# A gated GLU with a state-space branch on one core: first weight pair on two other rings, four pairs held back, and a start of single token tiles

## The chip, the cores and the metric

The kernel runs on one core of a Trainium2 chip. Times are device microseconds (us) of one execution. "Profiled span" is the time from the first to the last instruction in the one execution that was traced; the timed value is 1.7 to 2.1 us longer. TensorE's granted clock is recorded with each run (1.000 is full speed).

## The reference, cut to what matters

```python
xn = layernorm(x)                       # x: [2048 tokens, 576], bfloat16
glu = (sigmoid(xn @ w_gate) * (xn @ w_up)) @ w_down      # inner width 4608
# ... ssm: a diagonal complex state-space scan over the 2048 tokens
return x + ssm(xn) + glu
```

The gate, up and down products are most of the work, and all of it is TensorE's.

## The kernel before

Tokens come in blocks of 512 (four tiles of 128). The inner width comes in "groups" of 128 columns, and weights are loaded as pairs of groups: 288 KB of gate weights into the upper 64 partitions, 288 KB of up weights into the lower 64. 576 features are nine pieces of 64, so a group on one block is 18 matmuls of 64 rows, a gate and an up one side by side in the two halves of the array (in the trace of before 2628 of them fill 283.7 us, 108 ns each; the last warm-ups of 512 columns, over the whole array, come 216 ns apart).

The loads at the beginning. Two input tiles go on each of the SP and ACT rings (a ring is the queue on which one engine starts its DMA transfers); all weights, and block 1's input, go through GpSimd:

```python
for tt in range(TT_B):                                   # TT_B = 4: block 0
    load_x(tt, nc.sync if tt % 2 == 0 else nc.scalar)
for pr in range(2):
    load_wgu((0, pr), nc.gpsimd, nc.gpsimd)              # pairs 0 and 1
for tt in range(TT_B, 2 * TT_B):
    load_x(tt, nc.gpsimd, "hst")                         # block 1
dskip_rows = consts.tile([P, D], BF16, name="dskip_rows")
nc.gpsimd.dma_start(dskip_rows[:], A_Dskip.partition_broadcast(P))
for pr in range(2, 4):
    load_wgu((0, pr), nc.gpsimd, nc.gpsimd)              # pairs 2 and 3
```

The start, on block 0. Tiles are normalised, transposed on TensorE and copied to `xT` two at a time, and the first two groups are multiplied in 256-column halves:

```python
for tt in range(2):
    ln_stats(tt)
    ln_std(0, tt, tt + 1)
for tt in range(2):
    ln_recip(0, tt, tt + 1)
    ln_norm(tt, twice=False)
    start_transpose(tt)
busy(20, P)                                   # 20 warm-up matmuls on zeros
start_copy(0, slice(0, NH), nc.scalar.copy)
# ... cut: statistics of tiles 2 and 3, the copies of tile 1
start_groups[0].mms(slice(0, 2 * P))
start_transpose(2)
start_transpose(3)
start_groups[1].mms(slice(0, 2 * P))
# ... cut: the copies of tiles 2 and 3
for g in start_groups:
    g.mms(slice(2 * P, TB))
```

The order of the groups afterwards (`f` is the group, the second number the block), then the down-projection of both blocks, which reads `hT`, the product of a group's gate and up halves that VectorE writes. Block 1's input is normalised behind this and transposed by DMA:

```python
order = [(f, 0) for f in range(2, 8)] + [(f, 1) for f in range(0, 8)]
order += [(f, nb) for nb in range(2) for f in range(8, 12)]
```

## Time and profile before

| | before |
|---|---|
| time, median (range) of the runs that stand against the changed kernel | 509.75 us (508.93 to 509.82) |
| profiled span | 508.4 us |
| TensorE busy | 500.6 us |
| first gate/up matmul, first one of 512 columns | 8.63, 13.90 us |
| first down-projection matmul, end of the last matmul | 58.71, 504.46 us |

The page and the table of stretches are read in the prediction below. Two lines of the page that it did not show matter later: TensorE's granted clock in 40 slices of the span, in tenths, and the DMA queue that the page calls "instruction" (packets, MB, share of the 16 DMA engines).

```profile
PEclk9999999999999999999999999999999999999999
...
q8 instruction: 35, 0.57, 0.5%
```

The clock is whole wherever it is recorded, from 4.3 us on. (The page prints 9 before that too, but the first warm-up matmuls, of 512 columns, are 0.43 us apart, twice the later 0.216.) The second line looks like nothing: half a per cent of the DMA time.

### The profile page before, as it was taken

Reading aid. Unit: us, or ns where it says so; the run is one execution under the profiler, and the core shown is the slowest. Engines: PE = TensorE matmul, PEld = TensorE weight load, DVE = VectorE, ACT = ScalarE, POOL = GpSimd, SP = SyncE. Lnnn points to the kernel's source line nnn. Section 1 sums busy time; section 2 is a strip of 40 time slices with the busy share of each in tenths; the row PEclk is TensorE's granted clock in tenths of the full one; section 3 lists DMA queues with packets and bytes.
Section 4 is the critical chain, followed back from the end, with each engine's and each line's share of the span. In section 5 each row is a group of like instructions: output and inputs, shape, how many; then the busy total and the mean of one; then the engine's idle time right before and its main releaser. Section 6 shows DMA issues by size and latency. Waiting matters only on the chain.

```text
span 508.4 us, 10667 instructions
## 1 busy us (share of the span) xinstructions
PE 500.6 (98%) x4536; PEld 292.6 (58%) x4536; DVE 323.5 (64%) x703; ACT 204.6 (40%) x368; POOL 96.6 (19%) x143
## 2 busy tenths in 40 slices
PE   8989999999999999999999999999999999999996
PEld 5445676444477444467764444774444774446775
DVE  6964999977888587868688667786675222221111
ACT  4757642556500756530016655005655005553000
POOL 6147430133110043110001231100431001300000
PEclk9999999999999999999999999999999999999999
DMA  8997997075220098342340662200753201600001
GB/s 208 172 170 143 235 194 125 2 164 122 57 57 25 1 170 153 76 107 69 73 104 3 163 141 48 46 24 1 150 122 81 48 25 38 172 1 4 33 25 36
DMA packets 42960, 45.60 MB, mean 90 GB/s; under 512 B 30496, under 2 KB 34336, under 8 KB 42912
## 3 DMA queue, kind: packets, MB, share of 16 engines
q0 software_dynamic: 12672, 34.23, 31.7%
q1 hardware_dynamic: 29808, 10.33, 10.2%
q8 instruction: 35, 0.57, 0.5%
q10 hardware_dynamic: 432, 0.37, 0.2%
q14 instruction: 13, 0.11, 0.1%
HBM read 34.36 MB, written 2.36 MB: 72 GB/s over the span
## 4 chain that ended last, share of the span: by engine, by line
PE 94%; DVE 3%; DMA 1%; ACT 1%; issue 0%
PE pgu L488 52%; PE pd L562 35%; PE pbu L517 7%; DVE bnst L220 1%; DMA xT<-xn 1%; DVE xn L240 1%; DMA xt<-in_A_x_dram 1%; ACT xT L737 0%; DVE acc L263 0%; PE ptr L734 0%; DVE mv L221 0%; DVE tmpxd L260 0%; DVE hT L497 0%; DVE ob L571 0%; DVE xn L245 0%
## 5 line engine op out<-in xcount | busy, mean ns | idle before, releaser
L488 PE MATMUL pgu<-xT,wgu 64*128 64x512 bf16 (+1 forms) x2628 | 283.7, 373 | 1.8 <-DMA xT<-xn 1.8
L488 PEld LDWEIGHTS <-wgu 64*128 64x128 bf16 x2628 | 130.0, 94 | 150.7 <-issue 2.5
L562 PE MATMUL pd<-wd,hT 128*128 128x288 bf16 x1152 | 144.6, 286 | 0.0
L494 ACT ACTIVATE sT<-pgu 128x512 bf16<-128x512 f32 x144 | 86.5, 600 | 119.4 <-PE pgu L488 109.7
L562 PEld LDWEIGHTS <-hT 128*128 128x128 bf16 x1152 | 112.2, 98 | 30.7 <-issue 0.8
L497 DVE TENSOR_TENSOR hT<-sT,uT 128x512 bf16<-128x512 bf16 x144 | 60.5, 421 | 100.0 <-ACT uT L495 99.8
L495 ACT CAST uT<-pgu 128x512 bf16<-128x512 f32 x144 | 84.1, 584 | 0.0
L151 POOL DMA_DIRECT2D wgu<-in_B_w_gate_dram x36 | 27.7, 769 | 227.7 <-PE pgu L488 207.7
L523 ACT COPY bure<-pbu 128x512 f32<-128x512 f32 x16 | 9.4, 585 | 104.3 <-PE pbu L517 88.5
L157 POOL DMA_DIRECT2D wd<-in_B_w_down_dram x36 | 26.4, 735 | 100.6 <-PE pd L562 99.5
L582 DVE TENSOR_TENSOR acc<-acc,pd 128x576 f32<-128x576 f32 x32 | 23.9, 750 | 24.1 <-PE pd L562 24.1
L579 DVE TENSOR_TENSOR ob<-acc,pd 128x576 bf16<-128x576 f32 x15 | 11.3, 754 | 40.9 <-PE pd L562 40.9
L517 PE MATMUL pbu<-xT,bt 64*128 64x512 bf16 x288 | 33.7, 376 | 0.0
L562 PEld LDWEIGHTS <-hst 128*128 128x128 bf16 x288 | 28.2, 98 | 7.1
L151 POOL DMA_DIRECT2D wgu<-in_B_w_up_dram x36 | 26.7, 742 | 1.5 <-issue 0.8
L562 PE MATMUL pd<-ctre,hst 128*128 128x288 bf16 x128 | 26.6, 286 | 0.0
L562 PE MATMUL pd<-ctim,hst 128*128 128x288 bf16 x128 | 26.6, 286 | 0.0
L432 DVE TENSOR_TENSOR_SCAN gre<-r,g0re,wrim 128x512 bf16<-128x512 f32 x20 | 25.5, 1277 | 0.1
L517 PEld LDWEIGHTS <-bt 64*128 64x128 bf16 x288 | 13.7, 94 | 17.1 <-issue 0.9
L439 DVE TENSOR_TENSOR_SCAN gim<-r,g0im,wrim 128x512 bf16<-128x512 f32 x16 | 20.4, 1276 | 0.0
L220 DVE BATCH_NORM_STATS2 bnst<-xt 128x6 f32<-128x288 bf16 x32 | 12.5, 433 | 2.4 <-DMA xt<-in_A_x_dram 2.4
L419 DVE TENSOR_TENSOR tq<-T,buim 128x512 bf16<-128x512 bf16 x20 | 13.7, 684 | 0.0
(113 smaller groups left out, 273.9 us busy)
## 6 DMA issues: line engine op xcount, KB each, us to landing
wgu<-in_B_w_gate_dram POOLq DMA_DIRECT2D x36, 288.0 KB, 4.4
wgu<-in_B_w_up_dram POOLq DMA_DIRECT2D x36, 288.0 KB, 5.1
wd<-in_B_w_down_dram POOLq DMA_DIRECT2D x36, 288.0 KB, 6.2
out_dram<-ob SPq DMA_DIRECT2D x15, 144.0 KB, 1.8
xt<-in_A_x_dram SPq DMA_DIRECT2D x10, 144.0 KB, 2.6
xt<-in_A_x_dram POOLq DMA_DIRECT2D x4, 144.0 KB, 7.2
bt<-ctre POOLq DMA_DIRECT2D x2, 288.0 KB, 6.9
bt<-ctim POOLq DMA_DIRECT2D x2, 288.0 KB, 7.8
```

The source lines that it names most:

```text
L151: eng.dma_start(w[rows, :, :], src[:, fs].rearrange("(c p) f -> p c f", p=H))
L157: nc.gpsimd.dma_start(wd[:], B_w_down[f0:f0 + FP * P, :].rearrange("(n p) d -> p n d", p=P))
L220: nc.vector.bn_stats(st[:, gi, :], xt[:, gi * DH:(gi + 1) * DH])
L432: nc.vector.tensor_tensor_scan(gre[:], r_bc, w[:, 0, :], g0re[:, col], ALU.mult, ALU.add)
L439: nc.vector.tensor_tensor_scan(gim[:], r_bc, w[:, 1, :], g0im[:, col], ALU.mult, ALU.add)
L488: nc.tensor.matmul(self.ps[:, gi, cols], w[rows, c, fs], xT[self.nb][rows, c, cols], start=c == 0, stop=c == NH - 1)
L494: nc.scalar.activation(sT[:], self.ps[:, 0, :], ACT.Sigmoid)
L495: nc.scalar.copy(uT[:], self.ps[:, 1, :])
L497: nc.vector.tensor_mul(h[:], sT[:], uT[:])
L517: nc.tensor.matmul(out, w, xT[self.nb][rows, c, ts_], start=c == 0, stop=c == NH - 1)
L562: nc.tensor.matmul(out, lhsT, rhs[:, a * DH:(a + 1) * DH], start=i == 0, stop=i == n - 1)
L582: nc.vector.tensor_add(halves(acc[:]), halves(acc[:]), pd[:, :, 0:DH])
```

## The change

Its intent: the first useful matmul should come earlier, and the hole before block 1 should go. The first pair goes on the SP and ACT rings, behind block 0's input tiles. The next four pairs are held until tile 0's statistics are done, by a small write that VectorE makes into pair 1's buffer and that the load has to wait for. Tiles go through the start one at a time. Eight groups on block 0, not six, stand between the start and block 1. The fifth pair borrows the place of a table that is not needed yet.

```diff
+        if key == (0, 4):
+            w = consts.tile([P, NH, FP * P], BF16, name="wgu4", tag="T1")
+        # ... cut
+        if held:
+            nc.vector.memset(w[:, 0, 0:2], 0.0)
 ...
-    for pr in range(2):
-        load_wgu((0, pr), nc.gpsimd, nc.gpsimd)
+    load_wgu((0, 0), nc.sync, nc.scalar)
     for tt in range(TT_B, 2 * TT_B):
-        load_x(tt, nc.gpsimd, "hst")
+        load_x(tt, nc.sync, "hst")
 ...
+    def load_behind():
+        for pr in range(1, 5):
+            load_wgu((0, pr), nc.gpsimd, nc.gpsimd, held=pr == 1)
+        nc.gpsimd.dma_start(dskip_rows[:], A_Dskip.partition_broadcast(P))
 ...
+    ln_stats(0)
+    load_behind()
+    ln_std(0, 0, 1)
+    ln_stats(1, (0,))
+    start_norm(0)
+    start_transpose(0)
+    busy(14, P)
+    start_copy(0, CA, nc.scalar.copy)
+    # ... cut: the same for tiles 1 to 3, each tile's 128-column matmuls
+    #     on both groups between the transposes of the next tiles
 ...
-                order = [(f, 0) for f in range(2, 8)] + [(f, 1) for f in range(0, 8)]
-                order += [(f, nb) for nb in range(2) for f in range(8, 12)]
+                order = [(f, 0) for f in range(2, 10)] + [(f, 1) for f in range(0, 10)]
+                order += [(f, nb) for nb in range(2) for f in range(10, 12)]
# cut: prefetch counts for five pairs, side loads one step earlier in their round,
#      the state inputs asked for through the background list
```

More of the change, by code (lines that the diff above doesn't have):

```diff
@@ L144, with load_wgu @@
     wd_t = {}
-    def load_wgu(key, eng_g, eng_u):
+    def load_wgu(key, eng_g, eng_u, held=False):
         f0 = (key[0] % NC * (FC // FP) + key[1]) * FP * P
-        w = wpool.tile([P, NH, FP * P], BF16, name="wgu", bufs=4)
+        if key == (0, 4):
+            w = consts.tile([P, NH, FP * P], BF16, name="wgu4", tag="T1")
+        else:
+            w = wpool.tile([P, NH, FP * P], BF16, name="wgu", bufs=4)
+        if held:
+            nc.vector.memset(w[:, 0, 0:2], 0.0)
         fs = slice(f0, f0 + FP * P)
@@ L163 @@
         load_x(tt, nc.sync if tt % 2 == 0 else nc.scalar)
-    for pr in range(2):
-        load_wgu((0, pr), nc.gpsimd, nc.gpsimd)
+    load_wgu((0, 0), nc.sync, nc.scalar)
     for tt in range(TT_B, 2 * TT_B):
-        load_x(tt, nc.gpsimd, "hst")
+        load_x(tt, nc.sync, "hst")
     dskip_rows = consts.tile([P, D], BF16, name="dskip_rows")
-    nc.gpsimd.dma_start(dskip_rows[:], A_Dskip.partition_broadcast(P))
-    for pr in range(2, 4):
-        load_wgu((0, pr), nc.gpsimd, nc.gpsimd)
+    def load_behind():
+        for pr in range(1, 5):
+            load_wgu((0, pr), nc.gpsimd, nc.gpsimd, held=pr == 1)
+        nc.gpsimd.dma_start(dskip_rows[:], A_Dskip.partition_broadcast(P))
     eps_t = consts.tile([P, 1], FP32, name="eps_t")
@@ L210, with ln_stats @@
     ln_count = [0]
-    def ln_stats(tt):
+    bnst = {}
+    def ln_stats(tt, parts=(0, 1)):
         nb, tl = divmod(tt, TT_B)
-        if tl == 0:
+        if tl == 0 and 0 in parts:
             mvs[nb] = lnp.tile([P, TT_B, nc.vector.BN_AGGR_DIM], FP32, name="mv")
@@ L217, in ln_stats @@
         xt = xts[tt]
-        st = lnp.tile([P, 2, BN], FP32, name="bnst")
-        for gi in range(2):
+        if 0 in parts:
+            bnst[tt] = lnp.tile([P, 2, BN], FP32, name="bnst")
+        st = bnst[tt]
+        for gi in parts:
             nc.vector.bn_stats(st[:, gi, :], xt[:, gi * DH:(gi + 1) * DH])
-        nc.vector.bn_aggr(mvs[nb][:, tl, :], st[:])
+        if 1 in parts:
+            nc.vector.bn_aggr(mvs[nb][:, tl, :], st[:])
     def ln_std(nb, t0, t1):
@@ L309 @@
     c512, s512 = sc4[:, 3, :], sc4[:, 2, :]
-    T1 = consts.tile([P, NU, TB], BF16, name="T1")
+    T1 = None
     T2 = consts.tile([P, NU, TB], BF16, name="T2")
@@ L378, in tables @@
     def tables(pt, part):
+        nonlocal T1
+        if T1 is None:
+            T1 = consts.tile([P, NU, TB], BF16, name="T1", tag="T1")
         sb_, cb_ = sc_tab[(pt, 0)], sc_tab[(pt, 1)]
@@ L481, in open, with mms @@
             self.ps = ps_pair("pgu")
-        def mms(self, cols=slice(0, TB)):
+        def mms(self, cols=slice(0, TB), cs=range(NH)):
             w = wgu_t[(self.slot, self.f // FP)]
             fs = slice((self.f % FP) * P, (self.f % FP + 1) * P)
-            for c in range(NH):
+            for c in cs:
                 for gi, rows in ((0, slice(0, H)), (1, slice(H, P))):
@@ L656 @@
     all_pairs = [(s, p) for s in range(n_slots) for p in range(n_pairs)]
-    wgu_next = [4]
+    wgu_next = [5]
     wd_next = [0]
@@ L679, in used @@
             pairs_done[0] += 1
-            prefetch_wgu(pairs_done[0] + 4)
+            prefetch_wgu(max(pairs_done[0] + 4, min(pairs_done[0], 4) + 5))
         n_used = sum(v for k, v in uses.items() if k[0] == g.slot)
@@ L713, in run_groups @@
             used(g)
-            if side_loads and i % 3 == 2:
+            if side_loads and i % 3 == 1:
                 side_loads.popleft()()
@@ L737, in start_copy, with start_mms, start_norm @@
         eng(xT_tile(0)[:, cs, tt * P:(tt + 1) * P], ptrs[tt % 2][:, cs, :])
-    for tt in range(2):
-        ln_stats(tt)
-        ln_std(0, tt, tt + 1)
-    for tt in range(2):
+    def start_mms(g, tt, cs=range(NH)):
+        start_groups[g].mms(slice(tt * P, (tt + 1) * P), cs)
+    CA, CB = slice(0, 5), slice(5, NH)
+    def start_norm(tt):
         ln_recip(0, tt, tt + 1)
         ln_norm(tt, twice=False)
-        start_transpose(tt)
-    busy(20, P)
-    start_copy(0, slice(0, NH), nc.scalar.copy)
-    ln_stats(2)
-    start_copy(1, slice(0, 5), nc.scalar.copy)
-    ln_std(0, 2, 3)
-    ln_stats(3)
-    ln_std(0, 3, 4)
-    start_copy(1, slice(5, NH), nc.vector.tensor_copy)
-    for tt in range(2, TT_B):
-        ln_recip(0, tt, tt + 1)
-        ln_norm(tt, twice=False)
-    start_groups[0].mms(slice(0, 2 * P))
-    start_transpose(2)
-    start_transpose(3)
-    start_groups[1].mms(slice(0, 2 * P))
-    for tt in range(2, TT_B):
-        start_copy(tt, slice(0, 5), nc.scalar.copy)
-        start_copy(tt, slice(5, NH), nc.vector.tensor_copy)
-    for g in start_groups:
-        g.mms(slice(2 * P, TB))
+    ln_stats(0)
[6 more added lines that the diff above has]
+    start_copy(0, CA, nc.scalar.copy)
+    ln_stats(1, (1,))
+    ln_std(0, 1, 2)
+    start_copy(0, CB, nc.scalar.copy)
+    ln_stats(2, (0,))
+    for g in range(2):
+        start_mms(g, 0, range(0, 5))
+    start_norm(1)
+    start_transpose(1)
+    start_copy(1, CA, nc.scalar.copy)
+    for g in range(2):
+        start_mms(g, 0, range(5, NH))
+    ln_stats(2, (1,))
+    ln_std(0, 2, 3)
+    start_copy(1, CB, nc.scalar.copy)
+    ln_stats(3, (0,))
+    start_norm(2)
+    start_mms(0, 1)
+    start_transpose(2)
+    start_mms(1, 1)
+    ln_stats(3, (1,))
+    ln_std(0, 3, 4)
+    start_copy(2, CA, nc.scalar.copy)
+    start_copy(2, CB, nc.scalar.copy)
+    start_norm(3)
+    start_mms(0, 2)
+    start_transpose(3)
+    start_mms(1, 2)
+    start_copy(3, CA, nc.scalar.copy)
+    start_copy(3, CB, nc.vector.tensor_copy)
+    for g in range(2):
+        start_mms(g, 3)
     for tt in range(TT_B, 2 * TT_B):
@@ L805 @@
                 side_loads.extend(ct_loads)
+                bg.add(0.0, lambda: want_bu(0))
+                bg.add(0.0, lambda: want_bu(1))
                 for i in range(len(chain)):
                     queue_ssm(i)
-                want_bu(0)
-                want_bu(1)
             if slot == 2:
@@ L813 @@
             if slot == 0:
-                run_groups([GateUp(slot, f, nb) for (f, nb) in order[:6]])
+                run_groups([GateUp(slot, f, nb) for (f, nb) in order[:8]])
                 catch_up_ln(1)
-                order = order[6:]
+                order = order[8:]
                 side_loads.extend([load_consts] + bt_loads)
```

## The prediction

Passages that said more of the hardware than a trace of this case shows are cut from it. No term of its sum (+1.4 - 1.8 + 0.15, about -0.2 us) is among them. Two of its steps stand on what is left: "two run side by side" on the 108 ns of a 64-row matmul, where the last warm-ups of 512 columns over the whole array come 216 ns apart; and the 2.95 us of the first pair on my estimate that its two loads share some 200 GB/s, which is what GpSimd's loads moved in before (216 GB/s from 4.6 to 8.6 us). That the two rings interleave can be seen in the input tiles: from 2.5 to 3.5 us both queues move (q1 0.20 MB, q10 0.18 MB).

> **What bounds the kernel now.** I read the page first (busy shares, slices), then TensorE's waits, then a table of stretches, then the timeline of the first 28 us.
>
> ```profile
> PE 500.6 (98%) x4536; PEld 292.6 (58%) x4536; DVE 323.5 (64%) x703; ACT 204.6 (40%) x368; POOL 96.6 (19%) x143
> ...
> PE   8989999999999999999999999999999999999996
> ```
>
> TensorE is busy in every slice but a little less in slices 0, 2 and 39. The waits of TensorE (line, releaser, us in total, times, longest) say what those holes are:
>
> ```profile
> PE pgu L488 <- DMA xT<-xn: 1.8, 1, 1.8
> PE pgu L726 <- DVE warm L178: 1.3, 1, 1.3
> PE ptr L734 <- DVE xn L245: 0.7, 1, 0.7
> ```
>
> Three waits in the whole run, all before 28 us. The table by stretch (columns: length, then busy us and instruction count per engine, granted clock, DMA share, GB/s) puts a size on each part:
>
> ```profile
> 0.00:8.63 8.63, 6.61 (x73) 3.98 (x74) 5.09 (x20) 3.64 (x6) 6.51 (x15) 1.00 0.80 182
> 8.63:13.90 5.27, 5.27 (x108) 4.59 (x109) 4.01 (x12) 3.66 (x7) 3.56 (x6) 1.00 1.04 243
> 13.90:25.70 11.80, 11.80 (x112) 5.16 (x106) 11.16 (x25) 8.25 (x14) 0.28 (x4) 1.00 0.98 171
> 25.70:27.52 1.82, 0.03 (x3) 0.03 (x1) 1.78 (x5) 1.21 (x3) 0.00 (x0) 1.00 0.90 133
> 27.52:504.80 477.28, 476.94 (x4248) 278.82 (x4248) 301.32 (x645) 187.79 (x341) 86.28 (x119) 1.00 0.40 85
> 504.80:508.40 3.60, 0.00 (x0) 0.00 (x0) 0.14 (x1) 0.00 (x0) 0.00 (x0) 1.00 0.08 23
> ```
>
> From 27.52 us on TensorE has no hole until the last output, and the change neither adds nor takes matmul work there. So the time moves by two numbers only: the moment X at which the first two gate/up groups are finished (13.9 us now; the full 512-column groups start then), and the hole of 1.8 us at 25.7 us, where block 1's transposed input comes late. The 6.61 us of TensorE in the first row hide the third point: most of it is warm-up, the first useful gate/up matmul is at 8.63 us. No more than these can be won: (8.63 - about 7) + 1.8, some 3.5 us or 0.7%.
>
> The start itself, from the timeline:
>
> ```profile
> 3.59 0.82 DVE L220 BATCH_NORM_STATS2 bnst<-xt 128x6 f32<-128x288 bf16 x2 [2.40 <-DMA xt<-in_A_x_dram]
> ...
> 5.64 0.43 DVE L245 TENSOR_SCALAR xn<-xt,mv,rstd 128x576 bf16<-128x576 bf16 x1
> ...
> 6.86 1.71 ACT L737 COPY xT<-ptr 128x1152 bf16<-128x1152 bf16 x2 [0.95 <-PE ptr L734]
> ...
> 7.29 1.29 PE L726 MATMUL pgu<-warm 128*128 128x128 bf16 x20
> 8.63 1.16 PE L488 MATMUL pgu<-xT,wgu 64*128 64x256 bf16 x18
> ...
> 11.25 0.43 DVE L737 COPY xT<-ptr 128x512 bf16<-128x512 bf16 x1 [0.98 <-ACT xT L737]
> ```
>
> Two things let 8.63 go together. The ScalarE copies of tiles 0 and 1 end at 6.86 + 1.71 = 8.57. And the first pair's two weight DMAs, issued from GpSimd at 1.45 and 2.33, take 5.7 and 6.2 us to land (the tile's view, one DMA per window), so the second lands at about 8.55. The last line shows that a VectorE copy of one part waits for ScalarE's copy of the other.
>
> [...] 20 warm matmuls of 128 columns, each with its load, fill 1.29 us, one alone lasts 219 ns, so (1290 - 219)/19 = 56 ns. [...] 2628 gate/up matmuls of 64 rows fill 283.7 us, 108 ns each[...]: two run side by side. Whether two 64-row loads go side by side quickly enough for 128 columns, no row of before shows: at 256 columns a pair has 109 ns, which hides either. [...] the DMA view from 2 us in slices of 0.475 us shows 361, 386, 351 GB/s (the four input tiles), then 81 at 3.9 to 4.4 us although the gate weights had been issued at 1.45, then some 200.
>
> **Part 1, the first pair on SP and ACT, the rest held.** The input's data end at about 3.9 us. A 288 KB load at some 200 GB/s is 1.47 us; the two rings interleave, so the pair needs 2.95 us: data to 6.85, and with the 0.5 us that the input tiles took from data to landing, 7.2 to 7.4 us instead of 8.55. The held loads are issued at 4.65 at the earliest and start moving some 3 us later (as above), so they hardly disturb the pair. Block 1's input lands at about 9 us instead of 12 to 13.4, which nobody waits for: VectorE reaches it at 12.2 now. Pairs 1 to 4 are 4 x 2.95 = 11.8 us of transfer after that, landing at about 12, 15, 18 and 21; needed at X, X + 3.9, X + 7.8, X + 11.7. No wait.
>
> **Part 2, tiles one by one.** TensorE's work is the same: 144 half-array matmuls of 128 columns are 72 pairs x 56 ns = 4.0 us against 36 x 109 ns = 3.9 us. The start is then a chain through three engines, with durations of the same rows (stats 0.38 + 0.48 us, aggregate 0.13 to the next op, square root 0.30, reciprocal 0.15, normalise 0.43, 18 transposes 0.7 to the copy, ScalarE copies of 640 and 512 columns 0.70 and 0.60, 0.59 and 0.5 apart; 0.03 to 0.05 us per hand-over):
> - tile 0: stats 3.57, root 4.66, normalised 5.60, transposes 5.64 to 6.34, copy A 6.36 to 7.06. Matmuls on it from about 7.3.
> - tile 1: root 6.95 (ScalarE's order puts it behind copy A of tile 0), normalised 7.86, transposes 7.9 to 8.6, copies 8.62 to 9.97.
> - tile 2: root 9.2 to 9.5, normalised 10.1; TensorE's order puts the first group's matmuls on tile 1 ahead, until 10.25; transposes to 11.05, copies to 12.23.
> - tile 3: normalised 11.65, transposes behind tile 2's first matmuls: 12.6 to 13.3, copy A to 14.03, copy B on VectorE, behind it, to 14.48. Then the rest of group 0 and all of group 1 on tile 3: 0.75 us.
>
> So X is about 15.3, 1.4 us **later** than now, although the first useful matmul is 1.3 us earlier. Each tile costs a round of some 2.3 us through VectorE, ScalarE and TensorE; now tiles go two at a time and the copies are shared by two engines.
>
> **Part 3, block 1 later.** Eight groups on block 0 instead of six: block 1 is wanted at X + 8 x 1.96 = X + 15.7 = 31.0 instead of 25.7. Its statistics begin when VectorE leaves the start (14.4 instead of 12.2 us); from there to the landing of the last DMA transpose it now takes 27.4 - 12.2 = 15.2 us, so about 29.6. The 1.8 us hole goes, with 1.4 us to spare. Against it stands a small new one: group 5 needs the PSUM slot that group 1 leaves, and ScalarE empties that only after block 1's square root and two 1.28 us table loads: it ends at 19.07 now, the slot is wanted at 13.9 + 3 x 1.96 = 19.8, 0.7 us to spare. VectorE's freedom relative to X moves back by 0.85 us, so about 0.15 us of waiting.
>
> **Part 4, the fifth pair in T1's place, the state inputs queued, side loads one step on.** All in stretches without a hole; the tables want T1 after slot 0, from about 60 us, its pair is done at about 51. Worth 0.
>
> **Sum:** +1.4 (X) - 1.8 (hole) + 0.15 = about -0.2 us.
>
> **The rivals.** (a) The two 64-row loads of a pair take turns, so that a pair costs 107 ns at 128 columns too. For it: weight loads of 64x128 last 94 ns each. Against: the transposes and warm-ups fit 56 ns. Then X is some 1.0 us later still: +0.7 us. One in three. (b) The new start is as short as it was meant to be, because copies and roots interleave better than I add them up: X stays near 13.9 and the hole goes: -1.8 us, 508.0. What speaks against it is the chain above; one in six. (c) The first pair is slow on the rings, or held loads delay block 1's transposes so that a hole is left: +1 to +2 us, 511. One in ten.
>
> **Range and chances.** -0.2 with weight 0.4, +0.7 with 0.33, -1.8 with 0.17, +1.5 with 0.1 is a mean of 0.0 us; the likeliest single outcome is -0.2, and the runs of before scatter by 0.9 us below 509.82. Between them: prediction **509.7 us**, range 507.8 to 511.5. Two per cent is 10.2 us, three times all that the start offers: within 2% 0.98, faster 0.01, slower 0.01.
>
> **What would show it.** The TensorE wait for xT by DMA is gone. First gate/up matmul at 7.2 to 7.6. First 512-column matmul at about 15.3 (13.9 would be rival b, over 16 rival a). The start has several TensorE waits of 0.3 to 1 us for ScalarE copies and for normalised tiles. The last end of pair 4's loads at about 21 us, no wait for weights. From X + 16 on, the same 477 us without a hole. A difference over 3 us, or a hole after 35 us, would prove the picture wrong.

## The result, and the profile after

| | before | after |
|---|---|---|
| time, median (range), 4 runs each | 509.75 (508.93 to 509.82) | 516.3 us (515.22 to 518.63) |
| ratio of the fast runs, 95% interval | | 1.0138 (1.0102 to 1.0175) |
| mean granted clock in the profiled run | 1.000 | 0.996 (all four runs: 0.993 to 0.997) |
| first gate/up matmul | 8.63 | 9.22 us |
| first 512-column matmul | 13.90 | 20.90 us |
| first down-projection matmul | 58.71 | 64.57 us |
| end of the last matmul | 504.46 | 511.45 us |
| profiled span | 508.4 | 514.5 us |

Ratios, here and below, are the mean time of one kernel's fast runs over that of the other's of the same rounds, so not quite the ratio of the medians that are quoted. Executions over 1.5% slower than the fastest of the same kernel are left out of the means. 1.4% is inside the band of two per cent, but 516.3 lies 4.8 us above the range that was given.

First the page of after, the lines that answer to those of before:

```profile
span 514.5 us, 10800 instructions
...
PE   7799999999999999999999999999999999999997
...
PEclk9899999999999999999999999999999999999999
...
q8 instruction: 36, 0.59, 0.5%
```

Slice 1 (12.9 to 25.7 us) has lost TensorE time, and its clock was not whole. The waits of TensorE (line, releaser, us in total, times, longest) name the holes:

```profile
PE pgu L504 <- issue: 2.9, 1, 2.9
PE pgu L504 <- DMA wgu<-in_B_w_gate_dram: 1.7, 1, 1.7
PE pgu L742 <- DVE warm L186: 1.2, 1, 1.2
PE pd L578 <- DVE hT L513: 1.0, 1, 1.0
PE pgu L504 <- ACT xT L753: 0.8, 4, 0.2
```

The wait of 1.8 us for block 1's transposed input is gone, as intended. In its place stand 1.7 us for the first weights, four short waits for ScalarE's copies (0.8 together), 1.0 us in the down-projection, and the largest, 2.9 us, which the profile calls "issue": it sees nothing that TensorE waited for. The stretches (length, then busy us and count on PE, PEld, DVE, ACT, POOL, granted clock, DMA share, GB/s):

```profile
0.00:9.22 9.22, 6.24 (x49) 3.13 (x50) 4.76 (x18) 2.94 (x5) 5.82 (x17) 1.00 0.82 193
9.22:16.86 7.64, 6.81 (x175) 5.26 (x176) 2.51 (x9) 4.28 (x8) 2.33 (x4) 1.00 1.06 204
16.86:19.74 2.88, 0.00 (x0) 0.00 (x0) 2.40 (x9) 0.52 (x1) 0.00 (x0) 0.89 1.02 203
19.74:33.50 13.76, 13.76 (x133) 8.74 (x134) 11.54 (x23) 10.19 (x17) 0.00 (x0) 0.90 0.77 125
...
36.00:70.00 34.00, 33.03 (x301) 20.53 (x298) 20.37 (x50) 22.13 (x40) 21.05 (x31) 1.00 0.87 168
70.00:511.45 441.45, 441.45 (x3927) 258.98 (x3924) 279.41 (x591) 164.45 (x300) 64.14 (x87) 1.00 0.36 76
```

From 16.86 to 19.74 us TensorE does nothing at all, while the DMA engines are full (share 1.02). Then the clock is 0.90 on average: the clock records of this stretch give half speed for 3.41 us, from 19.1 us. Until about 22.6 us a pair of 128-column matmuls takes 107 ns and a pair of 512 columns 427 ns, twice what they take elsewhere (56 and 216). After 70 us TensorE has no hole, as in before.

The timeline of after around the hole (start, length, engine, line, operation, shapes, idle before):

```profile
15.39 0.69 ACT L753 COPY xT<-ptr 128x640 bf16<-128x640 bf16 x1 [1.11 <-PE ptr L750]
16.11 0.42 DVE L753 COPY xT<-ptr 128x512 bf16<-128x512 bf16 x1 [2.35 <-ACT xT L753]
16.13 0.73 PE L504 MATMUL pgu<-xT,wgu 64*128 64x128 bf16 x13 [0.18 <-ACT xT L753]
...
19.74 8.63 PE L504 MATMUL pgu<-xT,wgu 64*128 64x128 bf16 x83 [2.88 <-issue]
```

The last copy of the start ends at 16.53 us. Everything that the remaining matmuls need is there, and TensorE stops all the same after 13 of them.

The chain of waits of after, at its beginning (start, length, what), shows how the first pair's delay passes into the start:

```profile
1.66 7.51 DMA wgu<-in_B_w_gate_dram
...
9.22 0.73 PE pgu L504 x20
9.95 0.64 PE ptr L750 x18
```

The transposes of tile 1 stand behind the matmuls on tile 0 in TensorE's program, so they cannot begin until the first weights are there.

**Where the 7.0 us of TensorE's time went.** First 512-column matmul 20.90 instead of 13.90: +7.0. Those that ran at half clock until 22.6 us: (22.6 - 20.9) / 2, about +0.8. The hole before block 1: -1.8. The wait in the down-projection: +1.0. Together +7.0, which is the shift of the last matmul (511.45 - 504.46). The tail after it was 0.9 us shorter in this one execution.

### The profile page after: what moved, and what is told of

The parts are those of the page before. It is cut to its first block, busy times and chain, and to the rows that moved or that the text cites. A ratio compares the mean times of both kernels' runs of the same rounds, so it can differ in the third digit from the quotient of the medians.

```text
span 514.5 us, 10800 instructions
## 1 busy us (share of the span) xinstructions
PE 503.8 (98%) x4602; PEld 298.1 (58%) x4602; DVE 323.9 (63%) x702; ACT 206.1 (40%) x371; POOL 93.3 (18%) x137
## 4 chain that ended last, share of the span: by engine, by line
PE 93%; DVE 3%; DMA 1%; ACT 1%; issue 1%; SPq 0%
PE pgu L504 52%; PE pd L578 34%; PE pbu L533 7%; DMA wgu<-in_B_w_gate_dram 1%; DVE sctab L334 1%; DVE rnd L333 1%; DVE ang L358 1%; ACT xT L753 0%; DVE hT L513 0%; PE ptr L750 0%; ACT L337 0%; ACT uT L511 0%; ACT L510 0%; SPq L139 0%; ACT sT L510 0%
## 5 line engine op out<-in xcount | busy, mean ns | idle before, releaser
L504 PE MATMUL pgu<-xT,wgu 64*128 64x512 bf16 (+1 forms) x2700 | 286.7, 369 | 5.5 <-issue 2.9
L504 PEld LDWEIGHTS <-wgu 64*128 64x128 bf16 x2700 | 135.9, 95 | 151.1 <-issue 5.8
L598 DVE TENSOR_TENSOR acc<-acc,pd 128x576 f32<-128x576 f32 x32 | 24.0, 751 | 24.6 <-PE pd L578 24.6
```

Source lines behind the costliest of these rows:

```text
L504: nc.tensor.matmul(self.ps[:, gi, cols], w[rows, c, fs], xT[self.nb][rows, c, cols], start=c == 0, stop=c == NH - 1)
L598: nc.vector.tensor_add(halves(acc[:]), halves(acc[:]), pd[:, :, 0:DH])
```

## The experiments

All twelve kernels gave correct results. Each was timed beside the kernel before on the same chip; the times of before were 509.6 to 510.0 us in every job.

**Theories.** For the hole: either TensorE had *no instructions left*, because the next block of its program came late through full DMA engines (A), or some *wait that the profile doesn't show* lies in the new order of tiles, with the copies or the buffers of the transposes (B). For the rest: the chain of tiles, the late first pair, and the tail of the order each cost something by itself.

What led to A is the count of instructions. Queue q8 moves packets of 16384 bytes, 36 in after. I counted in the trace's records how many instructions TensorE had executed when each packet began (matmuls, weight loads and the few semaphore instructions, two of them at the very beginning): the k-th, from 0, at 192 + 256k, within 45 for all of them but the first. That is one packet for every 256 instructions, so I take a packet to be a block of 256 instructions of TensorE's program. I call the k-th due at 192 + 256k. Since 192 is 64 short of a block, I estimate that TensorE has some 64 instructions taken in ahead of those it has executed. The first packet was 257 late: it began when TensorE had executed 449 and stood still. 449 is 63 short of 512, by the same estimate the end of the second block. The "third block" and the "512 instructions" of the expectations below come from this estimate. These views of DMA in after (q0 carries GpSimd's loads) cover 10.7 to 16.6 us and 16.6 to 18.2 us (queue, packets, MB, share):

```profile
q0 software_dynamic: 387, 1.20, 103.5%
```

```profile
q0 software_dynamic: 105, 0.32, 101.2%
q8 instruction: 1, 0.02, 5.3%
```

The first has no instruction packet at all: weights have the engines. It moved at last in the second stretch, from 16.71 to 18.07 us by the DMA records, and TensorE went on at 19.74.

### part_order: the order alone

```diff
 # before, with
-    for pr in range(2, 4):
+    for pr in range(2, 5):          # fifth pair in T1's place, from GpSimd
 # and the new order, prefetch counts, side loads and queued state inputs
```

> The order alone on the kernel before: eight groups of block 0 ahead of block 1, the fifth pair in T1's place loaded last by GpSimd, side loads one step on, state inputs queued; loads and start as before. My theory of the slowdown puts all of it into the start (late first pair, an empty instruction queue, the half clock after it), so this part should show only the gain that was forecast for it: the 1.8 us hole before block 1 goes, first 512-column matmul stays at 13.9 us, total -1.8 us or a little less, about 508.1 us against 509.8. Rival: the order itself makes VectorE late for the first down-projection (the 1.0 us wait for hT at 68 us in the changed kernel); then that wait shows here too and the total is -0.8 us.

Measured: 509.32 us, ratio 0.9995 (0.9976 to 1.0013). The hole before block 1 is gone; in the traced run two waits stand in its place:

```profile
PE pgu L498 <- DMA wgu<-in_B_w_up_dram: 1.2, 1, 1.2
...
PE pd L572 <- DVE hT L507: 0.8, 1, 0.8
```

So in this run the order's gain of 1.8 us is given back: with the old loads pair 2 is late (it lands at 19.61 us), and the down-projection waits for `hT`. The traced run is the slowest of the four (510.82 us, the others 508.94 to 509.45), so the waits may be shorter in those. The second wait is in after too, so it belongs to the order and not to the tiles.

### part_loads: the loads alone

```diff
+    load_wgu((0, 0), nc.sync, nc.scalar)      # block 1's input on SP behind it
+    def load_behind(): ...                    # pairs 1 to 3 and dskip on GpSimd, held
 # called after the statistics of tile 0; old start, old order
```

> The loads alone on the kernel before: first pair on the SP and ACT rings, block 1's input behind it on SP, pairs 1 to 3 held on GpSimd until the first statistics; start two tiles at a time and order as before. Late weights: the pair lands at about 9.2 us as in the changed kernel, so the first gate/up matmul moves from 8.63 to about 9.2 us and the first 512-column one from 13.9 to about 14.5. Instructions: the third block of 256 is asked for at about the same time as in the changed kernel and its transfer starts only at 15 to 17 us instead of 12.1, but with 256-column matmuls TensorE has used only some 350 instructions by 14.5 us, so it does not run dry before it arrives, or for less than 1 us. Total +0.6 to +1.5 us. If the stall of 2.9 us and the half clock come with the loads whatever the tile size, +4 us or more.

Measured: 509.6 us, ratio 0.9997 (0.998 to 1.0013). The first pair lands at 9.02 (gate) and 8.23 us (up), so it is complete half a microsecond later than in before (8.5), and the first 512-column matmul is at 14.24. TensorE waits 0.8 us, until 27 us, for ScalarE to empty a PSUM slot (a place for a group's sums), where the hole before block 1 was. The instruction block waits almost as long as in after, from 10.29 to 15.68 us, but the trace has no "issue" hole: with the old tiles TensorE isn't through its instructions by then.

### part_tiles: the single tiles alone

```diff
 # before's loads and order
-    ...                       # two tiles at a time, 256-column matmuls
+    ...                       # after's start: one tile at a time, 128-column matmuls
```

> Tiles one by one alone on the kernel before: loads from GpSimd and order as before. The 128-column matmuls double the instructions before the full groups; by my theory the third block's fetch is delayed less here than in the changed kernel (it started at 12.1 us with these loads), so it lands by about 14 us and TensorE, which needs it only after 512 instructions, waits less than 1 us. First gate/up matmul at about 8.6 us, first 512-column one at 15.5 to 16.5. The hole before block 1 becomes smaller or stays: block 1's statistics start later by about as much. Total +1.5 to +3 us. If the stall belongs to the chain of tiles and not to instructions, the 2.9 us hole at tile 3 is here in full and the total is +4 us or more.

Measured: 513.7 us, ratio 1.0083 (1.0061 to 1.0105). The first gate/up matmul is at 8.01 us and the first of 512 columns at 16.84, 2.9 later than in before; both the start and the total cost more than I had expected. One of the four runs, 515.69 us at clock 0.996 and not traced, is in the ratio; the other three alone give 1.0075. Of TensorE's waits the longest is again the one for block 1:

```profile
PE pgu L493 <- DMA xT<-xn: 2.2, 1, 2.2
```

There is no "issue" hole. The order of tiles is that of after, so theory B would have expected one. What the three parts do to the time alone is about -0.3, -0.2 and +4.2 us (ratio minus one, times 509.8), +3.8 in sum; the whole change costs 7.0 by the same reckoning (ratio 1.0138). The rest of some 3 us comes only when the parts are *together*. That fits A, but these three runs do not show which parts it takes.

### split_before: twice the instructions, and nothing else

```diff
-    start_groups[0].mms(slice(0, 2 * P))
+    for t in range(2):
+        start_groups[0].mms(slice(t * P, (t + 1) * P))
 # likewise group 1 and the second half of both: 128 columns per matmul in before
```

> The kernel before with one thing changed: the eight 256-column passes of the start are split into sixteen of 128 columns, same order, same data, same loads; 144 instructions more before 14 us, some 0.3 us of array time more. Instruction theory: TensorE uses up its first 512 instructions at about 13.0 us; the third block, whose transfer ran from 12.1 to 13.2 us in the kernel before and can be used some 1.6 us after its end, comes at 14 to 15, so a hole of 0.7 to 1.9 us without any releaser appears in a kernel whose loads were not touched; total +0.8 to +2.2 us. If the hole in the changed kernel had another cause, there is none here and the total is +0.3 us at most.

Measured: 511.89 us (510.73 to 512.93), ratio 1.0037 (1.0016 to 1.0059). The list of TensorE's waits, then its timeline:

```profile
PE pgu L488 <- issue: 2.9, 1, 2.9
```

```profile
16.27 6.03 PE L488 MATMUL pgu<-xT,wgu 64*128 64x128 bf16 x61 [2.85 <-issue]
```

The hole of after appears in before, with before's loads, order of tiles, copies and buffers. TensorE stops after 449 instructions, the last begun at 13.2 us: the same count. Half clock follows here too (16.1 to 19.5 us). B falls: more instructions ahead of the start's end are enough to make the hole. In the start, before has 360 TensorE instructions (36 warm-ups, 72 transposes, 72 gate/up matmuls, each with its load), split_before 504 and after 492. The end of the second block, 512, is by the estimate above taken in when 449 are done. That lies beyond the start in before and inside it in the other two. The hole is longer than the 0.7 to 1.9 us that I expected, because the fetch began at 13.48 us, 1.4 later than in before, although it was due 0.7 earlier.

Two of the four timed runs were near 510.9 us at clock 0.999, two near 512.85 at 0.997, so the hole does not seem to be equally long every time; only one was traced.

### hold_more: the engines free when the block is due

```diff
     def load_behind():
-        for pr in range(1, 5): ...; dskip
+        load_wgu((0, 1), nc.gpsimd, nc.gpsimd, held=True)
+    def load_rest():                          # pairs 2 to 4, dskip
+        ...                                   # called after the statistics of tile 3
```

> The changed kernel with pairs 2 to 4 and the skip row held on GpSimd until tile 3's statistics (about 12.7 us); only pair 1 follows the first statistics. If the late instruction fetch comes from the DMA engines being full of held pairs when it is asked for (about 11 us), they now have nothing but pair 1 and block 1's input until 14 us: the fetch starts before 13.5 us instead of at 16.7, no hole of 2.9 us and no half clock; first 512-column matmul at 17.5 to 18, total about 512 us, 4 us better than the changed kernel. Pair 2 lands at about 18 and is wanted at about 21.5: no weight wait. Rival (the fetch is late because it is asked for late, whatever the engines carry): it starts at 16 us or later again and the total stays at 516.

Measured: 513.13 us, ratio 1.0059 (1.0042 to 1.0076). The DMA view of 11 to 13 us:

```profile
q0 software_dynamic: 55, 0.13, 32.6%
q8 instruction: 1, 0.02, 4.2%
```

The engines run empty here: over these two microseconds they are a third full. The block moves at 11.49 us, 0.4 us after its turn instead of 6.0, and no "issue" hole is left. The tiles and their 492 instructions are those of after. That is the second half of A: not the count alone, but the count and a late block. The first 512-column matmul still comes only at 18.22 us, because the first pair lands at 9.39; in the traced run half clock followed the wait for it (10.8 to 14.2 us). The other three runs had clock 1.000 and 512.6 to 513.17 us against 513.36, so half clock cost little here. The down-projection waits 0.7 us for its weights, which this edit moved back.

### more_warmups: the block asked for earlier

```diff
-    busy(10, TB)
+    busy(40, P)
-    busy(14, P)
+    busy(44, P)
```

> The changed kernel with MORE warm-up matmuls: the first ten of 512 columns become forty of 128 (same array time), the fourteen after tile 0's transposes become forty-four (they fill the wait for the first pair). 120 instructions more, all before 9 us, none of them needed. Instruction theory: the sequencer asks for the third block when it has used the first, now at about 6 to 7 us instead of about 11, so the transfer starts before 13 us, there is no hole of 2.9 us and no half clock at 17 to 22 us; total about 512.5 us, 3.5 to 4 us faster than the changed kernel. Rival (the hole is a hidden wait of the chain of tiles, or plain lack of instructions per microsecond): the hole stays or grows, 516 us or more.

Measured: 513.85 us, ratio 1.0076 (1.0059 to 1.0094). The same warm-up time in more instructions asks for the block at 8.46 us. It moves 4.1 us earlier than in after (12.61 instead of 16.71 us), the hole shrinks from 2.9 to 1.2 us, and there is no half clock. I had expected no hole. The sixty added instructions also bring TensorE to the end of its blocks sooner, and a second hole, 0.8 us long, ends at 24.6 us, behind the next fetch (21.87 to 23.06). It comes after 705 instructions, 256 more than 449: one block further, as A would have it.

### The blocks side by side

The first packet of q8 in eight traces, read from the DMA records. "Due" is when TensorE has executed 192 instructions. The last but one column is the start of the 449th.

| | due | fetch | wait | TensorE at 449 | hole |
|---|---|---|---|---|---|
| before | 9.93 | 12.08 to 13.19 | 2.2 | 18.23 | none |
| part_tiles | 10.27 | 12.26 to 13.73 | 2.0 | 16.17 | none |
| part_order | 10.26 | 14.16 to 15.45 | 3.9 | 20.10 | none |
| part_loads | 10.29 | 15.68 to 17.03 | 5.4 | 18.68 | none |
| hold_more | 11.08 | 11.49 to 12.83 | 0.4 | 17.55 | none |
| more_warmups | 8.46 | 12.61 to 13.96 | 4.1 | 14.12 | 1.2 |
| split_before | 9.27 | 13.48 to 14.81 | 4.2 | 13.21 | 2.9 |
| after | 10.74 | 16.71 to 18.07 | 6.0 | 16.65 | 2.9 |

TensorE goes on 1.5 to 1.7 us after a late fetch has ended. A hole opens in the cases, and only in those, where the fetch's end plus that 1.6 us is later than the 449th instruction. In part_loads it is 18.6 against 18.68: just in time. The same comparison for every later packet (35 or 36 per trace, each against an instruction count 256 higher), in all fourteen traces, foretells exactly one more hole, the second of more_warmups, and no trace has any other "issue" hole of more than 0.2 us.

### x_behind: block 1's input behind pair 1

```diff
-    for tt in range(TT_B, 2 * TT_B):
-        load_x(tt, nc.sync, "hst")
     def load_behind():
         # pair 1, then
+        for tt in range(TT_B, 2 * TT_B):
+            load_x(tt, nc.gpsimd, "hst")
```

> The changed kernel with block 1's input taken off the SP ring and loaded by GpSimd behind pair 1. If the first pair is late (9.2 us against a forecast of 7.3) because block 1's input shares the engines with it, it lands at 7.3 to 7.9 us and the chain of tiles begins 1.3 to 1.9 us sooner. The instruction hole is not cured by that: TensorE reaches the end of its 512 instructions sooner, the fetch waits behind the same pairs; so the hole stays, at least 2 us, and the total gains 0 to 1.9 us on the changed kernel (514.5 to 516.3). Rival: small rows on these two rings are slow by themselves; then the pair lands at 8.8 us or later again.

Measured: 511.76 us, ratio 1.0036 (1.0021 to 1.0051). Two of TensorE's waits:

```profile
PE pgu L505 <- DMA wgu<-in_B_w_gate_dram: 1.1, 1, 1.1
PE pd L579 <- DVE hT L514: 1.0, 1, 1.0
```

Block 1's input, on the same ring directly behind the first pair, costs the pair 0.8 us: it now lands at 8.38 instead of 9.17. One trace each would not be enough, for the landing varies by as much between kernels with the same early loads. But the four traces with block 1's input there have it at 9.0 to 9.4 us (9.2 on average), the six without at 7.7 to 8.5 (8.1). It was not all: the forecast of 7.2 to 7.4 us is still some 0.8 us off. The "issue" hole went as well, which I had not expected. The fetch, due at 9.95, begins at 12.12, a wait of 2.2 us, although the engines are as full meanwhile as in after (share 1.10 against 1.04). So what decides *how long* an instruction block waits behind the weights is not settled by the share alone. The record has a hint: by issue times and packet sizes I estimate that GpSimd had started loads of some 1700 KB that had not yet moved when the block was due in after, 1580 KB in part_loads, 840 KB in x_behind and 120 KB in hold_more, and the waits were 6.0, 5.4, 2.2 and 0.4 us. The other traces, with 600 to 1060 KB, have waits from 1.6 to 4.2 us that do not follow this order, so it is not shown. First 512-column matmul: 16.52.

### two_by_two, two_by_two_mended, one_by_one_mended: the chain by itself

These three use x_behind's loads and the new order; the first two have the old start, two tiles at a time.

```diff
 # two_by_two: x_behind with before's start, and the state constants loaded early
+        load_consts()                          # at the end of load_behind
 # two_by_two_mended
+                nc.gpsimd.dma_start(dskip_rows[:], ...)   # directly after block 1's input
+                consts_at[0] = bg.now          # only where block 1's groups begin
 # one_by_one_mended: the same two lines, with after's start
```

> An attempt at the better of both: the changed kernel's loads and order, but the old start (two tiles at a time, 256 columns, fewer instructions), block 1's input behind pair 1 on GpSimd, and the small state constants asked for right after the first loads instead of behind the sixth pair. First pair at 7.3 to 7.9 us, first gate/up matmul at about 8.6 (the copies of tiles 0 and 1 bind), first 512-column matmul at 13.9; no hole before block 1, or a slot wait below 0.5 us; no wait for hT at 62 us since VectorE makes its angle tables earlier; no empty instruction queue. Total 507.5 to 508.3 us, 1.5 to 2 us better than before. If the instruction fetch is late with these loads for any start, a hole of 1 us or more shows at about 18 us and the total is 509 or more.

Measured: 513.88 us, ratio 1.0069 (1.0048 to 1.009), from faults of my own edit: `dskip` came late, VectorE waited 2.5 us for it, and the constants let ScalarE begin its exponentials where TensorE needed it (3.0 us of waiting, until 37 us). That is the traced run, of 511.84 us at whole clock; the other three had 513.69 to 514.22 us at clock 0.996 to 0.997 and were not traced. It says nothing of the start but that the first 512-column matmul is at 13.99.

> The attempt two_by_two with its two own faults mended: the skip row is loaded right behind block 1's input (VectorE waited 2.5 us for it), and the exponentials on the state constants are released only four groups after block 1 begins, as before (released early they made ScalarE, which evacuates the groups, wait behind VectorE: a hole of 3.0 us at 37 us). First 512-column matmul at 14.0, no hole before block 1, no wait for hT near 62 us, since the constants have long landed. Total 1.3 to 1.9 us below the kernel before, about 508.3 against 510.0. If the order cannot pay at all (some wait always takes the hole's place), the total is within 0.5 us of before.

Measured: 509.82 us, ratio 0.9994 (0.9981 to 1.0007). The first 512-column matmul is at 14.51. I had hoped that the wait in the down-projection would go with the better place of the exponentials; it did not:

```profile
PE pd L574 <- DVE hT L509: 1.0, 1, 1.0
```

> The same loads, order and mending with the new start (tiles one by one, 128 columns): it differs from two_by_two_mended in the start alone. No hole by instructions (block 1's input behind pair 1 let the fetch through at 12.1 us), no hT wait. What is left is the chain of tiles that the prediction worked out: first pair at about 8.0, first 512-column matmul at 16.3 to 16.6, so 2.3 to 2.6 us above two_by_two_mended, and about 0.6 to 1.0 us above the kernel before (510.6 to 511.0). If the chain was not the cost and only the empty queue was, both versions take the same time.

Measured, where the clock was whole: 511.84, 511.91 and 512.8 us (three of six runs). The other three had 519.5 at clock 0.993, 519.87 and 524.27 us. The ratio 1.0078 (1.003 to 1.0125) contains the 519.5, so I compare the undisturbed runs alone: 2.1 us over two_by_two_mended by the medians (511.91 and 509.82), for the single tiles without a queue hole. In the traces the first 512-column matmul is at 16.11 against 14.51, 1.6 us. The forecast had +1.4 for this chain.

What the disturbed runs went through isn't known: none was traced. A late instruction block with half clock behind it would look like that, but that is only a guess.

### block0_done_early and block0_early_hold: the tail of the order

```diff
 # block0_done_early: two_by_two_mended with
-    order = [(f, 0) for f in range(2, 10)] + [(f, 1) for f in range(0, 10)]
-    order += [(f, nb) for nb in range(2) for f in range(10, 12)]
+    order = [(f, 0) for f in range(2, 10)] + [(f, 1) for f in range(0, 8)]
+    order += [(f, 0) for f in range(10, 12)] + [(f, 1) for f in range(8, 12)]
 # block0_early_hold: the same, with pairs 2 to 4 and the constants held
 # until the statistics of tile 3, as in hold_more
```

In the change only two groups of block 1 stand between block 0's last group and its down-projection; in before there are four. VectorE makes one `hT` every 1.9 to 2.2 us there, between the angles of the state tables, and is some groups behind TensorE: in after the `hT` of block 0's last group ends at 68.35 us, and the down-projection, begun at 64.57, reaches it after 22 matmuls.

> two_by_two_mended with one line of the order changed: block 0's last two groups (10 and 11) come after eight groups of block 1 instead of after ten, so four groups of block 1 follow them, as in the kernel before, instead of two. The wait of TensorE for hT came after 22 matmuls of the first down-projection, that is at its twelfth term, block 0's group 11: the change's order leaves that group 3.9 us less before the down-projection begins, while VectorE lags behind by its angle tables. If so, the 0.96 us wait goes and nothing takes its place: about 508.9 us against 510.0 of before, at last clear of it. If the lag of VectorE alone decides (tables later than before whatever the order), the wait stays at about 1 us and the total at 509.8.

Measured: 508.18 us (five runs 507.93 to 508.87, one 513.79 at clock 0.997, untraced), ratio 0.9988 (0.9953 to 1.0022). All of TensorE's waits in the traced run:

```profile
PE pgu L738 <- DVE warm L188: 1.2, 1, 1.2
```

With four groups behind it again, the wait is gone, and so is every other one behind the first warm-up. The interval is wide because of the one disturbed run.

> block0_done_early with pairs 2 to 4 held on GpSimd until tile 3's statistics (about 8.3 us). Five of six runs of block0_done_early lay at 507.9 to 508.9 us, one at 513.8 with a lower mean clock, as runs with an empty instruction queue have it. If that one was a late instruction fetch behind the held pairs, fewer pairs in the engines at 10 us make it rarer: all runs at 507.9 to 508.9, none with a clock of 0.997 or less, and the version is clear of before by 1.5 to 2 us. Pair 2 lands at about 16 us, wanted at 18. If the slow run had another cause, one of six may lie at 513 again; if pair 2 comes late, a weight wait of up to 1 us at 18 us takes the gain.

Measured: 508.33 us (five fast runs 508.09 to 509.01; one of 518.0 us is left out), ratio 0.9974 (0.9961 to 0.9987). By its fast runs this version beats both kernels, by 0.26% and 1.6% (0.9974 over 1.0138). With the slow run its mean is 510.0 us, no better than before's 509.8; before itself was never above 511.1 us in its 51 runs. The first 512-column matmul is at 13.85 us, as early as in before, and the span is 506.4. The held loads were meant to keep the engines free for the instruction block too; a run at low clock still came up once in six, with no trace of it, so whether they help with that is open.

## Why the prediction was wrong

**What was right.** The hole before block 1 went. In after that was partly luck: X was so late that block 1 began only at 37.2 us, against 31.0 in Part 3. With X at 14.51 (two_by_two_mended) eight groups were just enough, with 0.2 us of waiting before block 1 instead of 1.4 us to spare. The 64-row loads don't take turns: a pair of 128 columns takes 55 to 56 ns (rival a is out). The chain's own spacing held: the transposes of tiles 1, 2 and 3 begin at 9.88, 12.36 and 14.65 us in after, steps of 2.5 and 2.3 where Part 2 said "some 2.3 us", and the last copy begins at 16.11, 2.1 us later than forecast, the same shift as the first pair's. one_by_one_mended put the chain's cost at 1.6 to 2.1 us, near the +1.4 of the sum. No weight pair after the first kept TensorE waiting. From 70 us on TensorE had no hole.

**The step that failed most: "So the time moves by two numbers only", with X worked out from data and engines alone.** Part 2 counted TensorE's work in the start as the same ("144 half-array matmuls of 128 columns are 72 pairs x 56 ns = 4.0 us against 36 x 109 ns = 3.9 us"). The time is the same; the instructions are not. They are twice as many for this work, and the packets of TensorE's program (q8, which the page counts as a share of the same 16 DMA engines) come while Part 1 fills these engines with four pairs of weights: the first was due at 10.74 us and began at 16.71. TensorE ran dry for 2.88 us at the 449th instruction, which the change moved inside the start, and the idle time was followed by half clock, worth about 1.4 us (0.55 in the start's last matmuls, 0.8 in the first of 512 columns, from the pair times above). No rival of the prediction was of this kind. That it is the instructions is shown by split_before (their number alone makes the hole), by hold_more (the same instructions with the block early: no hole) and by the times of the blocks in all fourteen traces.

**Part 1, "7.2 to 7.4 us instead of 8.55".** The pair landed at 9.17. Rival (c) had named this, at one in ten. Some 1.1 us of the miss is block 1's input, which the change puts on the SP ring right behind the pair (9.2 us on average with it there, 8.1 without; 0.8 us in x_behind); the forecast let it share nothing. The rest, some 0.8 us, is not explained. The delay then passed whole into the chain, about 1.9 us, because TensorE's order puts tile 1's transposes behind tile 0's matmuls. Part 2 had the first matmuls at 7.3 and no wait for weights in front of them.

**Together for X:** 15.3 as forecast, +1.9 (pair), +2.9 (queue empty), +0.6 (half clock in the start) is 20.7; measured 20.90.

**The tail of the order, in none of the four parts.** Part 4 says of the later edits "All in stretches without a hole ... Worth 0", and the time was to move "by two numbers only". There was a third, 1.0 us: the order's last four groups were changed too, and block 0's last `hT` came too close to the down-projection. part_order has this wait without the new loads and tiles, block0_done_early removes it. Part 3 looked only at where block 1 begins, not at where block 0 ends.

**The sum** therefore read +1.4 - 1.8 + 0.15, and should have read +7.0 (X) + 0.8 (half clock after it) - 1.8 + 1.0; the slot wait of 0.15 did not show. The prediction's own alarm, "a difference over 3 us, or a hole after 35 us, would prove the picture wrong", rang on both counts.

**What stays open.** Why the block waited 6.0 us in after and 2.2 in x_behind with equally full engines (the loads queued ahead of it are a candidate, not shown); the remaining 0.8 us of the first pair; why half clock follows some holes and not others (it followed 2.9 us in after and in split_before and 2.2 us in hold_more, but not 2.2 us in part_tiles or 3.0 us in two_by_two); and what happens in the occasional slow runs at lower clock, which several of the changed versions have and before does not. None of these slow runs was traced.

## What to carry to other kernels

Count instructions and not only busy time when you cut matmuls into smaller ones near the beginning: here a DMA packet of 16384 bytes came for every 256 instructions of TensorE, and behind a burst of weight loads the first was held back for up to 6.0 us, with half clock after the two "issue" holes of 2.9 us. A wait called "issue" with no releaser, after 449 or 705 instructions (63 short of two and three times 256), is how this looked in the traces; holding loads back for a moment (hold_more) or fewer and wider matmuls (before) kept it away. And when an order of groups is changed, look at both ends of it: at the consumer that starts after the last group as well as at the input of the first.
